# One constant in a delta-rule and MLP kernel: the input projection's eleven-product form in the last four blocks of tokens, in place of the last two

## The chip, the cores and the metric

The kernel runs on one core of a Trainium2 chip. The metric is the device time of one execution in microseconds (us), as the median of several runs. Engines are named TensorE (PE in the profile; PEld is its weight load), VectorE (DVE), ScalarE (ACT), GpSimd (POOL) and SyncE (SP, which here only issues DMAs).

## What is computed

A delta-rule recurrence over 4 batches, 8 heads, 768 tokens and 48 channels, and then an MLP with the hard-swish activation on the 3072 tokens, all in float32:

```python
k_n = k / (norm(k) + 1e-6)
for t in range(S):
    y[:, :, t] = q[:, :, t] @ state
    v_old = state^T k_n[t]
    state = state + beta[t] * outer(k_n[t], v[t] - v_old)
x = y.transpose(0, 2, 1, 3).reshape(3072, 384)
h = x @ w_in                                  # 384 -> 2048
g = h * clip(h + 3, 0, 6) / 6
out = g @ w_out                               # 2048 -> 384
```

## The kernel before

**Tokens and blocks.** The recurrence goes in 24 chunks t of 32 tokens, all batches at once on the 128 partitions. Each chunk needs the inverse of a triangular matrix; the chunks 1 to 4, 5 to 8, ... 17 to 20 and 21 to 23 form groups 1 to 6, and the inverse of a group is found by substitution on VectorE (`inverse(g)`): a transpose in (L456), 30 pairs of a product (L746) and a subtraction (L751) of growing and then shrinking size (128x30 up to 128x240 and back to 128x30), a memset (L755) and a transpose out (L460). Two chunks make a block of 256 tokens, `blk = t // 2`, and there are 12 blocks.

**The recurrence of one chunk** (`chain(t)`) has on TensorE: ks (L793, the state times keys and queries), pz (L814, the inverse X times the residual R), su (L912, the update of the state), py (L814, output), and yt (L859, the transposes of the output y into xT). Between them VectorE makes R (L806), y (L806, L849) and the new state (L928), and ScalarE copies.

**The MLP of one block** is "up" and "down". `up(blk)` multiplies 16 column tiles of `w_in`, three products of 128x256 each (L968); ScalarE (L976) and VectorE (L979) apply the activation and write g. `down_by_seven(blk)` multiplies g by `w_out` in Strassen's form with seven products (L1196); VectorE makes the sums of g (L1182, four groups named A22, A21, A11, A12), and combines the products (L1206); ScalarE copies them out of PSUM (L1203). The last instruction of down on VectorE is an L1206 that reads the last product.

**`up_by_eleven(blk)`**, used for blocks from `UF` on, does the 2x2 part of the projection (two column tiles of `w_in`, two halves of the tokens, the first two thirds of the 384 channels) in Strassen's form with seven products, and the last third plainly with four: eleven products of 128x128 (L1039) for each pair of column tiles, eight pairs to a block, where `up` has six of 128x256. It needs sums of `w_in` (`weight_sums`, 16 instructions on GpSimd, L1005, made during the down of block `UF - 1`; one of the sums overwrites tiles of `w_in`), and sums of x (`token_sums`, four instructions on VectorE, L1029, called T1x, T2x, T3x and T4x below; T1x is made first and used by the second product). For each pair of tiles, `begin` issues four products, a copy of them out of PSUM to g on ScalarE (L1053), and three additions on GpSimd (L1005); `end` issues the other seven products, two additions on VectorE (L1069, L1070), and then ScalarE's copy (L1076) and relu (L1080, into a buffer ro that shares its place with the output tile o) and VectorE's product (L1083), the last a pair behind.

**The order of the work** is written out by hand. From chunk 5 on each chunk has 15 units; in a unit u, `plan[u]` issues the next part of the recurrence, then one piece of the MLP (`units`: 14 for a down, 16 for an up), then evictions, then steps of the substitution (`fill`). So block 8's up runs beside chunk 18, its down beside chunk 19, block 9's up beside chunk 20, its down beside chunk 21, and inverse(6) is begun in chunk 18 and must be whole before pz of chunk 21. The lines that use the constant or follow from it:

```python
sums = weight_sums() if blk == UF - 1 else iter(())                     # L1284
(up_by_eleven if blk + 1 >= UF else up)(blk + 1)                        # in L1290
12: lambda: token_sums(t // CB) if t % CB and t // CB >= UF else None,  # L1435
take(fill, 1 if mode["slow"] else 2 + (u % 3 == 0))
```

`mode["slow"]` is set while an `up_by_eleven` runs, and what is left of a substitution when the next group of chunks begins is issued in one go (`drain(fill)`). Each engine works through its own instructions in that order.

Of the kernel before, what the change touches and what calls it, by code (L numbers as in the profile page):

```python
# [46 lines left out]
def kernel(  # L47
# [942 lines left out]
                past.add(("up", blk))  # L990
            yield

    UF = 10
    S1, S2, S4 = (sums_in[:, i] for i in range(3))

    def w_tiles(s, i):
# [10 lines left out]
    def weight_sums():  # L1007
        for j in range(0, NPR, 2):
            r = slice(j, j + 2)
            plus_minus(S1[:, r], W21[:, r], W22[:, r], ALU.add)  # L1010
            yield
            plus_minus(S2[:, r], S1[:, r], W11[:, r], ALU.subtract)
            yield
            plus_minus(S4[:, r], W12[:, r], S2[:, r], ALU.subtract)
            yield
            plus_minus(W21[:, r], W11[:, r], W21[:, r], ALU.subtract)
            yield
# [5 lines left out]
    def token_sums(blk):  # L1023
        needs(("seam", blk * CB), ("seam", blk * CB + 1), ("up", blk - 1))
        B11, B12, B21, B22, _, _ = (
            x.rearrange("p (a b) -> p a b", b=16) for x in x_tiles(blk)
        )
        for out, a, b in ((T1x, B12, B11), (T2x, B22, T1x), (B12, B22, B12), (T4x, B21, T2x)):
            nc.vector.tensor_tensor(out=out, in0=a, in1=b, op=ALU.subtract)  # L1029
        past.add(("sums", blk))  # L1030
# [230 lines left out]
    def mlp_units():  # L1261
# [10 lines left out]
        def downs(blk):  # L1272
            if blk >= FIRST:
                yield from down_by_seven(blk)
                return
            for c in range(CB):
                for f in range(0, NFC, WF):
                    if c == 0:
                        needs(*(("read", ("ph", blk, f + i, None)) for i in range(2)))
                    down(blk, c, f)  # L1280
                    yield

        for blk in range(1, N // CB):
            sums = weight_sums() if blk == UF - 1 else iter(())  # L1284
            for _ in downs(blk):
# [3 lines left out]
            if blk + 1 < N // CB:  # L1289
                for n, _ in enumerate((up_by_eleven if blk + 1 >= UF else up)(blk + 1)):  # L1290
                    if blk + 1 == FIRST and n >= HF:
# [10 lines left out]
    def take(gen, n=1):  # L1302
        for _ in range(n):
            while next(gen, None) == 1:
                pass
# [91 lines left out]
    with tc.manual_schedule():  # L1397
# [12 lines left out]
        for t in range(LS, N):  # L1410
# [11 lines left out]
            if i == 2:  # L1422
# [11 lines left out]
                11: lambda: take(ch),  # L1434
                12: lambda: token_sums(t // CB) if t % CB and t // CB >= UF else None,  # L1435
                13: lambda: take(later),
# [56 lines left out]
```

## Time and profile before

| what | value |
|---|---|
| time, median of 3 runs | 687.84 us (685.55 to 689.42) |
| time of the profiled execution | 685.55 us |
| its span, first to last instruction | 683.8 us |
| TensorE busy | 647.7 us (95%) |
| TensorE weight loads busy | 572.6 us (84%) |
| VectorE busy | 475.2 us (69%) |
| ScalarE busy | 253.3 us (37%) |
| GpSimd busy | 118.3 us (17%) |
| mean granted TensorE clock | 0.990 |

The span is the time from the first to the last instruction; 1.75 us lie around it. Shares of busy time are means over stages of different kinds, so the stages are read one by one. In the tables below a line such as "L1039 PE MATMUL ph<-xT,w_in" means that line 1039 issues a product on TensorE that writes the tile ph from xT and w_in; in a timeline the first number is the start in us from the start of the span, the second the duration, and a bracket at the end gives the idle time before the instruction and who ended it. A float32 product of TensorE counts as two records.

### The profile page before, as it was taken

To read this page: it belongs to the slowest core of one execution; us is meant where nothing else is said; L and a number is where in the kernel's file an instruction comes from. 1 tells how busy PE (TensorE), PEld (TensorE's weight loads), DVE (VectorE), ACT (ScalarE), POOL (GpSimd) and SP (SyncE) were. 2 spreads that over 40 slices of the span, in tenths; PEclk is the share of its full clock that TensorE was granted. 3 is DMA by queue.
4 is the path that set the end of the run, shared out by engine and by line. 5 is a ranking of instruction groups with operands and counts; after the bars stand their busy time and mean duration, and the time that the engine had idled before them with its cause. 6 is when DMAs were issued, how large, how long until landed. Compare 5 with 4: busy or idle time off the path is not lost.

```text
span 683.8 us, 25829 instructions
## 1 busy us (share of the span) xinstructions
PE 647.7 (95%) x11368; PEld 572.6 (84%) x11368; DVE 475.2 (69%) x1234; ACT 253.3 (37%) x503; POOL 118.3 (17%) x200
## 2 busy tenths in 40 slices
PE   2588989999999999999999999999999999999997
PEld 2468977776689989989988988978988989999997
DVE  5888867898556996746985746985546995457354
ACT  5986776423133133232133132132232132143250
POOL 6240232002311100100100101102000032040230
PEclk9997999999999999999999999999999999999999
DMA  7995435402040030041030030020020020100000
GB/s 182 246 215 132 99 88 130 80 4 45 23 86 14 3 72 2 3 89 19 2 71 2 3 71 2 2 61 2 3 47 2 3 48 2 28 11 2 25 1 23
DMA packets 88496, 33.23 MB, mean 49 GB/s; under 512 B 80160, under 2 KB 83232, under 8 KB 88384
## 3 DMA queue, kind: packets, MB, share of 16 engines
q1 hardware_dynamic: 88128, 31.29, 20.5%
q8 instruction: 89, 1.46, 0.9%
q10 hardware_dynamic: 256, 0.30, 0.2%
q14 instruction: 23, 0.19, 0.1%
HBM read 26.84 MB, written 4.72 MB: 46 GB/s over the span
## 4 chain that ended last, share of the span: by engine, by line
PE 78%; DVE 16%; issue 2%; ACT 2%; DMA 1%; SPq 0%; POOL 0%; DVEq 0%; ACTq 0%
PE ph L968 28%; PE po L1196 22%; PE ph L1039 6%; PE po L1131 4%; PE pt L513 3%; PE ks L793 3%; DVE g L1182 3%; PE py L814 3%; PE su L912 3%; PE pz L814 2%; DVE A L751 2%; DVE pr L746 2%; PE sc L534 2%; PE yt L859 1%; PE pi L671 1%
## 5 line engine op out<-in xcount | busy, mean ns | idle before, releaser
L968 PE MATMUL ph<-xT,w_in 128*128 128x256 f32 (+1 forms) x1056 | 227.4, 368 | 3.4 <-DVE g L979 2.8
L968 PEld LDWEIGHTS ph<-xT,w_in 128*128 128x128 f32 x1056 | 185.3, 194 | 27.7 <-DVE g L979 3.9
L976 ACT ACTIVATE g<-ph,halves 128x256 f32<-128x256 f32 (+1 forms) x176 | 79.1, 453 | 165.5 <-PE ph L968 163.4
L979 DVE SCALAR_TENSOR_TENSOR g<-g,ph 128x256 f32<-128x256 f32 (+1 forms) x176 | 68.1, 391 | 67.4 <-ACT g L976 67.2
L1196 PE MATMUL po<-w_out,g 128*128 128x192 f32 x640 | 112.1, 326 | 0.0
L1196 PEld LDWEIGHTS po<-w_out,g 128*128 128x128 f32 x640 | 104.7, 190 | 0.4
L1196 PE MATMUL po<-spare,g 128*128 128x192 f32 x480 | 86.7, 332 | 0.0
L1196 PEld LDWEIGHTS po<-spare,g 128*128 128x128 f32 x480 | 77.2, 190 | 1.8
L1182 DVE TENSOR_TENSOR g<-g 128x256 f32<-128x256 f32 x160 | 65.7, 459 | 3.3 <-PE po L1196 3.2
L473 POOL TENSOR_TENSOR mb<-beta_tok,mask 128x256 f32<-128x256 f32 x38 | 25.9, 702 | 236.8 <-DVE LB L545 236.8
L751 DVE TENSOR_TENSOR A<-A,pr 128x30 f32<-128x30 f32 (+9 forms) x150 | 53.7, 358 | 3.4
L746 DVE TENSOR_TENSOR pr<-A 128x30 f32<-128x30 f32 (+9 forms) x150 | 52.0, 347 | 3.1
L348 ACT ACTIVATE spare<-spare,places 128x768 uint16<-128x768 uint16 (+1 forms) x56 | 52.4, 940 | 2.9 <-DMA spare<-in_moe_w_in_dram 2.0
L1131 PE MATMUL po<-w_out,g 128*128 128x384 f32 x128 | 45.6, 493 | 0.0
L1203 ACT ACTIVATE o<-po 128x192 f32<-128x192 f32 x40 | 13.2, 330 | 82.4 <-PE po L1196 82.4
L521 ACT ACTIVATE KQ<-pt 128x512 f32<-128x512 f32 x48 | 28.1, 594 | 29.6 <-PE pt L513 29.2
L1039 PE MATMUL ph<-xT,w_in 128*128 128x128 f32 x224 | 34.2, 278 | 0.2
L497 POOL TENSOR_TENSOR kb<-kf,inv 128x384 f32<-128x384 f32 x24 | 22.3, 930 | 66.2 <-PE yt L859 35.6
L1131 PEld LDWEIGHTS po<-w_out,g 128*128 128x128 f32 x128 | 23.2, 190 | 12.4
L1005 POOL TENSOR_TENSOR g<-g 128x128 f32<-128x128 f32 x48 | 21.8, 455 | 67.8 <-ACT g L1053 65.3
L863 ACT ACTIVATE xT<-yt 128x384 f32<-128x384 f32 x24 | 11.7, 486 | 57.2 <-PE yt L859 57.2
L793 PEld LDWEIGHTS ks<-state,KQ 64*64 64x64 f32 x1472 | 24.8, 138 | 8.6 <-issue 7.7
(137 smaller groups left out, 779.7 us busy)
## 6 DMA issues: line engine op xcount, KB each, us to landing
kf<-in_k_dram SPq DMA_DIRECT2D x96, 48.0 KB, 2.7
qb<-in_q_dram SPq DMA_DIRECT2D x96, 48.0 KB, 2.9
vf<-in_v_dram SPq DMA_DIRECT2D x96, 48.0 KB, 2.1
out_dram<-o SPq DMA_DIRECT2D x92, 48.0 KB, 1.6
spare<-in_moe_w_in_dram SPq DMA_DIRECT2D x4, 768.0 KB, 7.6
w_out<-in_moe_w_in_dram SPq DMA_DIRECT2D x4, 768.0 KB, 7.1
w_out<-in_moe_w_out_dram SPq DMA_DIRECT2D x4, 768.0 KB, 6.6
spare<-in_moe_w_out_dram SPq DMA_DIRECT2D x4, 768.0 KB, 4.8
```

What stands on the lines that cost most here:

```text
L348: nc.scalar.activation(out=z, in_=z if n else d.bitcast(I16)[:, :, :, 3], func=func, bias=places[:, n : n + 1], scale=scale,)
L746: nc.vector.tensor_tensor(out=pv, in0=A[:, j + 1 :, j].unsqueeze(2).to_broadcast([n, w, j]), in1=A[:, j, 0:j].unsqueeze(1).to_broadcast([n ...
L751: nc.vector.tensor_tensor(out=A[:, j + 1 :, 0:j], in0=A[:, j + 1 :, 0:j], in1=pv, op=ALU.subtract)
L793: nc.tensor.matmul(ph[y][c, e, D * p : D * p + D], lhsT=KQ[r, p * B // 2 + b // 2, 2 * y : 2 * y + 2, :].rearrange("k y c -> k (y c)"), rh ...
L814: nc.tensor.matmul(ps[rows(place(b)), D * h : D * h + D], lhsT=m(h)[rows(b)], rhs=z[rows(b), D * h : D * h + D], start=True, stop=True, sk ...
L968: nc.tensor.matmul(ph[:, cols], lhsT=w_in[:, s, f * 128 : (f + 1) * 128], rhs=xT[:, s, cols], start=(s == 0), stop=(s == NKT - 1),)
L976: nc.scalar.activation(out=g, in_=ph, func=ACTF.Relu, bias=half, scale=1.0 / 6.0)
L979: nc.vector.scalar_tensor_tensor(out=g, in0=g, scalar=1.0, in1=ph, op0=ALU.min, op1=ALU.mult)
L1039: nc.tensor.matmul(ph[:, n], lhsT=w, rhs=x, start=start, stop=stop, skip_group_check=True)
L1131: nc.tensor.matmul(pos[c][:], lhsT=gs[blk, f // 2][:, f % 2, c * P : (c + 1) * P], rhs=w_out[:, f, :], start=(f == 0), stop=(f == NFC - 1),)
L1182: nc.vector.tensor_tensor(out=A(f, *out), in0=A(f, *a), in1=A(f, *b), op=op)
L1196: nc.tensor.matmul(ps[n][:], lhsT=A(f - f % 2, *a)[:, f % 2], rhs=b[:, f], start=(f == 0), stop=(f == HF - 1),)
```

## The change

The constant UF goes from 10 to 8:

```diff
@@ -990,7 +990,7 @@
                 past.add(("up", blk))
             yield
 
-    UF = 10
+    UF = 8
     S1, S2, S4 = (sums_in[:, i] for i in range(3))
```

With it, blocks 8 and 9 go through `up_by_eleven` in place of `up`; `weight_sums` is made during the down of block 7 in place of block 9; `token_sums` is made for blocks 8 and 9 too, in unit 12 of the chunks 17 and 19, one unit behind the last unit of a down; and the substitution of group 6 goes at one step a unit while block 8's and block 9's ups run. Nothing else is edited.

## The prediction

> **What bounds the kernel now.** TensorE is busy for 95% of the span. So I first read the table of stages, cut where TensorE goes from one block's first projection ("up", L968 or L1039) to its output projection ("down", L1196). Columns: length, then busy time and instruction count of TensorE, its weight loads, VectorE, ScalarE, GpSimd; granted clock; DMA.
>
> ```profile
> core 0: us, PE busy (x) PEld busy (x) DVE busy (x) ACT busy (x) POOL busy (x), PEclk, DMA share, GB/s
> ...
> 498.27:523.44 25.17, 25.17 (x358) 21.56 (x357) 11.90 (x28) 8.45 (x18) 0.00 (x0) 1.00 0.15 34
> 523.44:546.08 22.64, 22.64 (x373) 21.70 (x371) 20.82 (x64) 3.58 (x9) 0.00 (x0) 1.00 0.00 1
> 546.08:571.24 25.16, 25.16 (x356) 21.55 (x356) 21.45 (x55) 8.45 (x18) 9.38 (x13) 1.00 0.16 34
> ...
> 593.88:619.09 25.21, 24.62 (x438) 23.70 (x436) 13.23 (x34) 11.73 (x24) 10.86 (x24) 1.00 0.11 26
> ```
>
> These are up(8), down(8), up(9) and up(10). Three things are to be seen. TensorE fills every stage, so a stage lasts as long as its products. up(10), already in the form with eleven products, takes 25.21 us, no less than the plain up(8) with 25.17. And VectorE is nearly full in down(8), 20.82 of 22.64 us: that is inverse(6), the substitution of the last tokens.
>
> Why eleven products gain nothing, the timeline of TensorE at the start of up(10) tells (start, duration, what it waited for in brackets):
>
> ```profile
> 593.88 0.38 PE L1039 MATMUL ph<-xT,w_in 128*128 128x128 f32 x2
> 594.79 0.46 PE L1039 MATMUL ph<-beta_tok,sums_in 128*128 128x128 f32 x2 [0.52 <-DVE beta_tok L1029]
> 595.32 0.46 PE L1039 MATMUL ph<-xT,w_in 128*128 128x128 f32 x2
> ```
>
> A product of 128 columns then starts every 0.2233 us (11 in 2.456 us, 649.40 to 651.86), one of 256 columns every 0.433 us (six in 2.60 us, 520.84 to 523.44). 88 x 0.2233 = 19.65 against 48 x 0.433 = 20.78: 1.13 us less. But the second product waits for x's first sum (L1029), and VectorE makes that only after the last addition of the output (L1206): the first three products take 1.73 us (593.88 to 595.61) for 0.67, 1.06 lost. The rest goes in changes between instruction kinds.
>
> **Part by part.** In the two builds' orders, TensorE, ScalarE and GpSimd have up(8) and up(9) exactly in the shape of up(10), with the recurrence at the same places; SP's queue is the same.
>
> *Up(8), by the row of up(10): 25.21 - 25.17 = +0.04.* Its VectorE queue holds no substitution ahead of x's sums (down(7) has none). The transpose A<-L (1.97 us) falls into the idle 1.08 us ahead of a group's additions; the next group absorbs the rest. The 24 added additions on GpSimd (0.456 us each), the 24 copies and relus on ScalarE and the 8 x 3 VectorE instructions stand in up(10) beside TensorE, at no cost beyond the 25.21. ro and the output tile share one buffer, but the output's DMAs are issued as early as in up(10).
>
> *Down(8): VectorE starts late.* The plain up leaves VectorE free, so the first ten steps of the substitution ran at 523.19 to 526.53, ahead of the recurrence's R. With eleven products up's last VectorE instruction (L1083) starts 2.47 us after down's first product and lasts 0.60 (621.56 against 619.09, in up(10)). So the steps start at 523.48 + 3.07 = 526.55, and with 2.77 us (their pitches below) R is at 529.32, where it was at 527.23: 2.09 us late. Does that wash out?
>
> ```profile
> 523.19 0.20 DVE L746 TENSOR_TENSOR pr<-A 128x30 f32<-128x30 f32 x1
> ...
> 526.23 0.30 DVE L751 TENSOR_TENSOR A<-A,pr 128x130 f32<-128x130 f32 x1
> 527.23 0.74 DVE L806 SCALAR_TENSOR_TENSOR R<-ks,parity,vf 128x192 f32<-128x192 f32 x2 [0.70 <-PE ks L793]
> ...
> 542.05 0.55 DVE L849 TENSOR_TENSOR y<-y,py 128x384 f32<-128x384 f32 x1
> ...
> 546.45 0.35 DVE L1206 TENSOR_TENSOR o<-u,po 128x192 f32<-128x192 f32 x1
> 546.72 0.40 DVE L751 TENSOR_TENSOR A<-A,pr 128x238 f32<-128x238 f32 x1
> 547.16 0.40 DVE L746 TENSOR_TENSOR pr<-A 128x234 f32<-128x234 f32 x1
> 547.59 0.40 DVE L751 TENSOR_TENSOR A<-A,pr 128x234 f32<-128x234 f32 x1
> ```
>
> No: after 527.23 no wait is listed until 567.73. VectorE runs without a gap through down(8), so 2.09 us of lag reaches its end. In the new order, x's sums of block 9 stand where the instruction at 547.59 stands. Three effects:
>
> 1. y of token 19 ends at 542.60 + 2.09 = 544.69; its transposes (yt) are due at 544.45 + 0.04 and start 0.15 after y (443.34 + 0.55 to 444.04): 544.84, **+0.35**.
> 2. up(9)'s first product: 546.08 + 0.04 + 0.35 = 546.47. T1x starts at 547.59 + 2.09 = 549.68 and the second product 0.43 later (594.36 to 594.79), at 550.11: 3.64 us behind the first, where up(10) has 0.91. **+2.73**, and +0.05 for the stage (25.21 - 25.16).
> 3. The Strassen sums of down(8) (L1182) are late too, but have 3 to 4 us to spare (A12 ends at 540.37 + 2.09, read at 544.78): nothing.
>
> *Up(9) and down(9).* In up(9) substitution goes at one step a unit, 17 steps beside the additions; ten more, a memset and a transpose come at the end in one go. From the time of T1x on, by the rows of up(10): last L1083 ends at +27.8, the steps 2.77, memset and transpose 1.95, R 1.3: +33.8. TensorE, whose down(9) starts at +24.73, wants pz 9.17 later (580.41 - 571.24), at +33.9: **+0.1** for the latency. So the thinned substitution just fits.
>
> *GpSimd's weight sums* move from beside up(9) to beside up(7) and the start of down(7), 16 x 0.73 us; bkb of the last token, which nothing reads, is queued behind them. They stretch VectorE's two-input steps: one took 0.86 us at 551.98 beside them, its neighbours 0.33 to 0.37. In up(7) that makes VectorE some 2 us later around 467; y of token 16 (due by 471.04, made at 468.98) then ends near 470.9: 0 to +0.3, I take 0.
>
> [...]
>
> *The clock.* Effect 2 leaves TensorE idle from about 546.85 to 550.11, 3.26 us. What such a gap does, earlier windows of this trace show: 1.79 us idle (46.75 to 48.54, longest wait 1.79), and then
>
> ```profile
> 46.50:49.93 3.43, 1.64 (x101) 1.29 (x96) 3.29 (x6) 3.37 (x5) 2.12 (x5) 0.99 0.92 260
> 49.93:53.34 3.41, 2.79 (x67) 2.31 (x66) 3.34 (x6) 3.11 (x5) 0.00 (x0) 0.50 0.41 70
> 53.34:56.75 3.41, 3.41 (x17) 3.41 (x18) 3.03 (x13) 0.73 (x2) 0.00 (x0) 0.51 0.98 258
> ```
>
> the clock is halved for 6.8 us. After 1.66 us idle (91.34 to 93.00) it was halved from 94.2 to 97.7, while 1.18 us idle (454.5) did nothing. 3.26 us idle puts at least 1.63 into one stretch of 3.4 us. Ends: 0, and two stretches, 3.4 us; I take one stretch of 3.41 us at half clock, **+1.7**, nearest to the 1.66 us row.
>
> [...]
>
> **Sum.** 0.04 + 0.35 + 2.73 + 0.05 + 0.1 + 1.7 = +4.97 us. The profiled execution took 685.55 (span 683.8 and 1.75 around it), so 690.5 for it; it is the fastest of three, the median being 687.84. I set the sum on the middle of the two, 686.7: **691.7**.
>
> **Rivals.** (a) The clock stays up: +3.27, 690.0. For it: 1.18 us idle did nothing. Against: two gaps of 1.66 and 1.79 us both halved it. 0.23. (b) The lag is absorbed, because up(8)'s tail is shorter than up(10)'s or VectorE's waits give way: +0 to +1.5, some 687.5. Against it, VectorE's 40 us without a wait. 0.13. (c) GpSimd's additions hold up the 17 steps of up(9) by 0.51 us each (0.86 - 0.35), 8.7 us, where VectorE has 6.2 to spare (27.8 less 14.6 for x's sums, the additions and the recurrence, less 17 x 0.41): pz another 2.5 late, +7.5, 694.2. Against: GpSimd works only 60% of that time. 0.08. (d) The other side: x's sums of both blocks come early enough, so that each block keeps the 1.13 us: -2.3, 684.4. It decides if T1x is made before down's last product ends; the order of VectorE puts it behind, and up(10) and up(11) both waited. 0.04. My forecast: 0.52.
>
> **How the numbers follow.** Half a per cent (3.4 us, about what a measurement of this kernel can tell from no change) puts the bounds at 684.4 and 691.3. Slower: forecast, (c), a little of (a): 0.60. Faster: (d), 0.04. Same: 0.36. Range: from the middle of (b), 687.0, to past (c) and two slow stretches (695), 696.
>
> **What would show it.** Right: the second product of up(9) waits about 3 us for L1029 and the granted clock is 0.5 for some 3.4 us after it; up(8) takes about 25.2 us; R in down(8) comes 2 us later; pz of down(9) hardly waits. Wrong: a gap below 1.5 us at up(9), which would mean that VectorE had caught up; a full clock after the gap; or waits inside up(9), (c).

## The result, and the profile after

| | before | after |
|---|---|---|
| median, us | 688.4 (683.82 to 692.34, 20 runs) | 693.49 (688.65 to 697.9, 20 runs) |
| ratio after/before, 95% interval | | 1.0074 (1.0051 to 1.0098) |
| profiled execution, us | 685.55 | 689.89 |
| its span, us | 683.8 | 687.8 |
| mean granted TensorE clock | 0.990 | 0.985 |

The change makes the kernel slower by 0.74%, some 5 us. The forecast was slower, 691.7 us in a range of 687 to 696.

The table of stages of after, cut as that of before (length; busy time and count of TensorE, its weight loads, VectorE, ScalarE, GpSimd; clock; DMA). The lines are up(8), down(8), up(9), down(9) and up(10):

```profile
core 0: us, PE busy (x) PEld busy (x) DVE busy (x) ACT busy (x) POOL busy (x), PEclk, DMA share, GB/s
497.97:523.17 25.20, 24.61 (x437) 23.69 (x436) 15.02 (x35) 11.73 (x24) 10.97 (x24) 1.00 0.15 34
523.17:546.12 22.95, 22.84 (x373) 21.66 (x372) 21.03 (x64) 4.83 (x11) 0.00 (x0) 1.00 0.01 2
546.12:575.13 29.01, 25.98 (x437) 25.10 (x436) 20.82 (x57) 11.73 (x24) 11.03 (x24) 0.94 0.14 30
575.13:597.77 22.64, 22.64 (x373) 21.71 (x372) 17.30 (x49) 4.94 (x11) 0.00 (x0) 1.00 0.01 1
597.77:622.98 25.21, 24.65 (x437) 23.70 (x436) 12.88 (x34) 11.53 (x24) 10.90 (x24) 1.00 0.11 27
```

Against before, up(8) took 0.03 more, down(8) 0.31 more, up(9) 3.85 more, and down(9) and up(10) nothing. The tail after up(11) took 0.11 more (22.22 for 22.11). Together this is 4.3 us. Nine tenths of it stand in one stage, and the clock column shows the same stage: 0.94 in the mean.

TensorE at the start of up(9) in after (start, duration, bracket with idle time and releaser):

```profile
544.46 0.52 PE L859 MATMUL yt<-ident,y 128*128 128x128 f32 x3
...
546.12 0.38 PE L1039 MATMUL ph<-xT,w_in 128*128 128x128 f32 x2
549.53 0.79 PE L1039 MATMUL ph<-beta_tok,sums_in 128*128 128x128 f32 x2 [3.02 <-DVE beta_tok L1029]
550.15 0.77 PE L1039 MATMUL ph<-xT,w_in 128*128 128x128 f32 x2
```

The second product starts 3.41 us behind the first, after 3.02 us of idle time that ends with x's first sum. And the second and third product last 0.77 to 0.79 us, where before's up(10) had 0.46. That is the halved clock, which a cut of this stage into three parts shows:

```profile
546.12:549.40 3.28, 0.39 (x4) 0.19 (x2) 3.04 (x10) 0.00 (x0) 0.00 (x0) 1.00 0.06 16
549.40:552.82 3.42, 3.29 (x14) 3.20 (x15) 1.48 (x6) 0.60 (x1) 0.69 (x2) 0.50 0.37 100
552.82:575.13 22.31, 22.31 (x421) 21.71 (x420) 16.30 (x42) 11.14 (x23) 10.34 (x23) 1.00 0.11 21
```

One stretch of 3.4 us at half clock follows the idle stretch, then it is whole again.

Where x's sum was, VectorE's timeline in after tells, at the beginning and at the end of down(8):

```profile
525.64 0.69 DVE L1083 SCALAR_TENSOR_TENSOR g<-o,g 128x512 f32<-128x512 f32 x1 [0.85 <-ACT o L1080]
526.25 0.20 DVE L746 TENSOR_TENSOR pr<-A 128x30 f32<-128x30 f32 x1
...
528.96 0.74 DVE L806 SCALAR_TENSOR_TENSOR R<-ks,parity,vf 128x192 f32<-128x192 f32 x2
```

```profile
548.17 0.35 DVE L1206 TENSOR_TENSOR o<-u,po 128x192 f32<-128x192 f32 x1
548.44 0.40 DVE L751 TENSOR_TENSOR A<-A,pr 128x238 f32<-128x238 f32 x1
548.87 0.40 DVE L746 TENSOR_TENSOR pr<-A 128x234 f32<-128x234 f32 x1
549.19 0.28 DVE L1029 TENSOR_TENSOR beta_tok<-xT 128x128 f32<-128x128 f32 x1
```

The last L1083 of up(8) holds up the first ten steps of the substitution, and these hold up R, which starts 5.79 us into the stage (528.96 - 523.17) where before it was 3.79 (527.23 - 523.44): 2.00 us late. At the end of the stage x's first sum, T1x, stands behind the output's last addition and two more steps of the substitution, at 549.19.

**How executions are compared here.** The stages from about 370 us to the end of down(7) last the same in every profiled execution of this case, to 0.03 us. What lies before them does not: the first of these stages began between 369.59 and 375.02 us in the ten kernels, whose edits all act later. So single profiled spans differ by up to 5 us for no reason in the edit. Below, the stages from up(8) on are compared, and the whole time by the ratio from several runs.

### The profile page after: what moved, and what is told of

Its sections match the earlier page's. It is cut to its first block, busy times and chain, and to the rows that moved or that the text cites. A ratio compares the mean times of both kernels' runs of the same rounds, so it can differ in the third digit from the quotient of the medians.

```text
span 687.8 us, 26297 instructions
## 1 busy us (share of the span) xinstructions
PE 645.7 (94%) x11528; PEld 575.8 (84%) x11528; DVE 485.7 (71%) x1258; ACT 262.9 (38%) x519; POOL 140.3 (20%) x248
## 4 chain that ended last, share of the span: by engine, by line
PE 73%; DVE 19%; ACT 3%; issue 2%; DMA 1%; SPq 1%; DVEq 0%; ACTq 0%
PE ph L968 22%; PE po L1196 19%; PE ph L1039 12%; PE po L1131 4%; DVE g L1182 3%; DVE A L751 3%; DVE pr L746 3%; PE ks L793 3%; PE pz L814 2%; PE py L814 2%; PE su L912 2%; PE pt L513 2%; PE sc L534 2%; ACT spare L348 2%; DVE o L1206 1%
## 5 line engine op out<-in xcount | busy, mean ns | idle before, releaser
L968 PE MATMUL ph<-xT,w_in 128*128 128x256 f32 (+1 forms) x864 | 184.2, 366 | 5.3 <-DVE g L979 2.9
L968 PEld LDWEIGHTS ph<-xT,w_in 128*128 128x128 f32 x864 | 149.9, 195 | 24.9 <-DVE g L979 3.9
L976 ACT ACTIVATE g<-ph,halves 128x256 f32<-128x256 f32 (+1 forms) x144 | 64.2, 450 | 131.9 <-PE ph L968 131.8
L1196 PEld LDWEIGHTS po<-w_out,g 128*128 128x128 f32 x640 | 104.5, 190 | 0.3
L979 DVE SCALAR_TENSOR_TENSOR g<-g,ph 128x256 f32<-128x256 f32 (+1 forms) x144 | 55.0, 386 | 51.6 <-ACT g L976 51.3
L1005 POOL TENSOR_TENSOR g<-g 128x128 f32<-128x128 f32 x96 | 43.8, 458 | 145.7 <-ACT g L1053 140.6
L1039 PE MATMUL ph<-xT,w_in 128*128 128x128 f32 x448 | 70.0, 280 | 0.3
L1039 PEld LDWEIGHTS ph<-xT,w_in 128*128 128x128 f32 x448 | 59.7, 194 | 1.5 <-issue 0.8
L1053 ACT ACTIVATE g<-ph 128x512 f32<-128x512 f32 x32 | 19.1, 597 | 50.5 <-PE ph L1039 50.5
L1069 DVE TENSOR_TENSOR g<-ph,g 128x128 f32<-128x128 f32 x32 | 9.2, 289 | 36.1 <-POOL g L1005 22.4
```

What stands on the lines that cost most here:

```text
L968: nc.tensor.matmul(ph[:, cols], lhsT=w_in[:, s, f * 128 : (f + 1) * 128], rhs=xT[:, s, cols], start=(s == 0), stop=(s == NKT - 1),)
L976: nc.scalar.activation(out=g, in_=ph, func=ACTF.Relu, bias=half, scale=1.0 / 6.0)
L979: nc.vector.scalar_tensor_tensor(out=g, in0=g, scalar=1.0, in1=ph, op0=ALU.min, op1=ALU.mult)
L1005: nc.gpsimd.tensor_tensor(out=out, in0=a, in1=b, op=op)
L1039: nc.tensor.matmul(ph[:, n], lhsT=w, rhs=x, start=start, stop=stop, skip_group_check=True)
L1196: nc.tensor.matmul(ps[n][:], lhsT=A(f - f % 2, *a)[:, f % 2], rhs=b[:, f], start=(f == 0), stop=(f == HF - 1),)
```

## The experiments

The theory: the loss is one wait, at up(9)'s second product, and the halved clock that it brings. It has two causes: x's sums stand behind the addition that reads down's last product in VectorE's queue, and VectorE comes 2 us late to down(8). The rivals: GpSimd's 24 additions beside VectorE are what costs; or the clock has nothing to do with it and the wait alone does it; or the eleven products can't be had more cheaply than twelve. All times of stages are in us:

| kernel | up(8) | down(8) | up(9) | down(9) | up(10) | up(11) | ratio to before (95%) |
|---|---|---|---|---|---|---|---|
| before | 25.17 | 22.64 | 25.16 | 22.64 | 25.21 | 20.77 | 1 |
| after | 25.20 | 22.95 | 29.01 | 22.64 | 25.21 | 20.77 | 1.0074 (1.0051 to 1.0098) |
| e3_filler | 25.20 | 22.95 | 27.80 | 22.65 | 25.20 | 20.77 | 1.0025 (1.0005 to 1.0044) |
| e4_uf9 | 25.17 | 22.64 | 26.12 | 22.65 | 25.20 | 20.76 | 1.0009 (0.9991 to 1.0026) |
| e1_sums_ahead | 24.15 | 22.93 | 25.93 | 22.64 | 24.16 | 19.72 | 0.9971 (0.9950 to 0.9992) |
| e2_no_lag | 25.20 | 22.64 | 29.00 | 22.65 | 25.20 | 20.77 | 1.0044 (1.0024 to 1.0064) |
| e7_spread | 25.75 | 22.64 | 26.36 | 22.64 | 25.21 | 20.77 | 1.0029 (1.0010 to 1.0048) |
| e5_both | 24.70 | 22.65 | 26.71 | 22.64 | 24.16 | 19.72 | 0.9978 (0.9950 to 1.0006) |
| e6_sums_ahead_uf10 | 25.16 | 22.64 | 25.16 | 22.64 | 24.16 | 19.72 | 0.9964 (0.9940 to 0.9987) |
| e8_late | 24.15 | 22.65 | 25.00 | 22.65 | 24.15 | 19.72 | 0.9962 (0.9938 to 0.9987) |

Each was made from the changed kernel, but e6_sums_ahead_uf10 from the kernel before.

### e3_filler: the same wait with TensorE kept busy

```diff
-            mm(ph, 0, W11[:, j], B11, start=True)
+            for _ in range(14 if blk == 9 and j == 0 else 1):
+                mm(ph, 0, W11[:, j], B11, start=True)
```

The first product of up(9) is issued 14 times.

> The changed kernel, with the first product of up(9) issued 14 times instead of once (each run starts the sum anew, so that the value is the same). It fills the wait for T1x with 13 x 0.223 = 2.9 us of products that need nothing new. Theory (the wait lowers the clock): the second product starts at the same time as in the changed kernel, the granted clock stays at 1.00, up(9) takes 29.0 - 1.3 = 27.7 us, the time is the kernel before's +3.5 to +4 us. Rival (the products after the wait are slow for another reason, such as their reads): they are at 0.42 us again with work ahead of them, up(9) takes 29 us, +5 us.

TensorE's timeline in e3_filler, and the first 6.8 us of its up(9) in two halves:

```profile
548.21 3.29 PE L1039 MATMUL ph<-xT,w_in 128*128 128x128 f32 x28
551.62 0.49 PE L1039 MATMUL ph<-beta_tok,sums_in 128*128 128x128 f32 x2
552.24 0.46 PE L1039 MATMUL ph<-xT,w_in 128*128 128x128 f32 x2
```

```profile
548.21:551.62 3.41, 3.29 (x30) 3.10 (x29) 3.13 (x11) 0.00 (x0) 0.00 (x0) 1.00 0.08 22
551.62:555.03 3.41, 3.28 (x26) 3.12 (x27) 1.39 (x5) 1.19 (x2) 1.24 (x3) 1.00 0.38 100
```

The second product is 3.41 us behind the first, exactly as in after, but now the clock stays at 1.00: 26 records in the second half, where after had 14 at half clock. up(9) takes 27.80 for 29.01. So of the 3.85 us, 1.21 were the clock, and the rest, 2.64, is the wait with what else differs in the stage. It also shows that the idle time, and not the late sum as such, lowered the clock: the sum was as late here, and the clock 1.00 for after's 0.50. By the ratios e3_filler lies 0.49% below after, some 3.4 us where the stage gives 1.21. The two ratios are uncertain by about 0.2% each, so this is at the edge of what they allow; the sums by stage against before, 3.0 and 4.3 us, lie inside the two intervals.

### e4_uf9: block 9 alone

```diff
-    UF = 8
+    UF = 9
```

up(8) stays plain; up(9) has its eleven products.

> UF = 9: block 9 in the eleven-product form, block 8 plain as in the kernel before. Theory: without up(8)'s additions VectorE begins the substitution as early as in the kernel before, so down(8) has no lag, and T1x stands only behind the two steps queued between it and the last L1206: the second product of up(9) starts 1.9 us behind the first (wait 1.5 us), up(9) takes 26.2 us with a whole clock, 27.5 with a halved one, and down(8) 22.64. Time +1.1 us against the kernel before, or +2.4 where the clock falls (1.2 us idle did not lower it, 1.66 us did). Rival (each block in this form costs the same): half of the change's loss, +2.5 us, with a wait as in up(10), 0.5 us.

TensorE at the start of up(9) in e4_uf9, and the stage:

```profile
547.95 0.38 PE L1039 MATMUL ph<-xT,w_in 128*128 128x128 f32 x2
549.77 0.46 PE L1039 MATMUL ph<-beta_tok,sums_in 128*128 128x128 f32 x2 [1.44 <-DVE beta_tok L1029]
```

```profile
547.95:574.07 26.12, 24.61 (x436) 23.69 (x436) 19.46 (x52) 11.74 (x24) 10.99 (x24) 1.00 0.15 33
```

With up(8) plain VectorE is on time: R starts 3.79 us into down(8), as before (529.10 - 525.31), and down(8) takes its 22.64. The second product still comes 1.82 us behind the first, 0.91 more than in up(10): 0.74 of these are the two steps of the substitution that stand between the last L1206 and T1x in chunk 19, and not in chunk 21 (1.02 us from the one to the other for 0.28), and 0.17 come from the last L1206, which starts that much later behind the first product. The other 1.59 of after's 3.41 come from the lag: T1x starts 26.02 us into down(8) in after (549.19 - 523.17) and 24.03 in e4_uf9 (549.34 - 525.31), 1.99 late. The later first product of up(9) has taken 0.31 of it, and the second product followed T1x by 0.34 us here and by 0.43 there. And 1.44 us of idle time left the clock whole (1.00) in this execution. The time is the same as before, within what is measured.

### e1_sums_ahead: x's sums one unit earlier

```diff
-                11: lambda: take(ch),
-                12: lambda: token_sums(t // CB) if t % CB and t // CB >= UF else None,
+                11: lambda: (take(ch), token_sums(t // CB) if t % CB and t // CB >= UF else None),
```

> The changed kernel, with x's sums (L1029) put one unit earlier, ahead of the last unit of the down instead of behind it, in all four blocks with eleven products. Theory (the loss is the wait for the first sum T1x, and the half clock that follows the long wait in block 9): the waits of 0.5 us in up(8), up(10) and up(11) go, about 0.9 us each with the slow restart, 2.7 us in all; in up(9) T1x is made some 1.9 us earlier, so that the wait falls from 3.0 to about 1.2 us and the clock stays whole, 1.9 + 1.3 us. Against the kernel before: +5 - 2.7 - 3.2 = about -1 us, each up near 24.3 us and up(9) near 25.8. Rival (the form with eleven products is itself slower, by its small products and more work on the other engines): the ups stay at 25.2 and 29 and the time at +4 to +5 us.

TensorE at the start of up(8), and the second product of up(9), in e1_sums_ahead:

```profile
502.06 0.38 PE L1039 MATMUL ph<-xT,w_in 128*128 128x128 f32 x2
502.28 0.39 PE L1039 MATMUL ph<-beta_tok,sums_in 128*128 128x128 f32 x2
...
550.68 0.49 PE L1039 MATMUL ph<-beta_tok,sums_in 128*128 128x128 f32 x2 [1.15 <-DVE beta_tok L1029]
```

In up(8), up(10) and up(11) the wait is gone, and each gains 1.05 us: the second product follows 0.22 us behind the first. So that wait was what ate the gain of eleven products. In up(9), where VectorE comes late, 3.02 us of waiting became 1.15, and the clock stayed whole (1.00 in the stage): 25.93. down(8) keeps its extra 0.3. One line moved turns a loss of 5 us into a gain of 2. The 24 additions on GpSimd are all still there in up(8), beside 24.15 us: they are not what costs there, and that rival falls. (In up(9), where the substitution runs beside them, they stretch its steps, as the next run shows.)

### e2_no_lag: no substitution right ahead of x's sums, two steps a unit later

```diff
-                if i == 1 == ready[0] and 5 < u < 12:
+                if i == 1 == ready[0] and 5 < u < 12 or t == 19 and 7 < u < 13:
                     continue
-                take(fill, 1 if mode["slow"] else 2 + (u % 3 == 0))
+                take(fill, 1 if mode["slow"] and t < 19 else 2 + (u % 3 == 0 and not mode["slow"]))
```

In chunk 19 no steps go in the units 8 to 12, and from there on two go in each unit of block 9's up. The ten steps ahead of R stay where they are.

> The changed kernel, in which the substitution of group 6 makes no step in units 8 to 12 of chunk 19, ahead of x's sums of block 9, and two steps a unit in chunk 20 in place of one. Theory (VectorE's lag through down(8) makes T1x late): VectorE has caught up when down(8) ends, T1x comes as early as in up(10), the wait at the start of up(9) is 0.5 us, the clock stays at 1.00, up(9) takes 25.2 to 25.6 us, and the time is the kernel before's +0 to +1 us. Rival (GpSimd's additions hold up VectorE's steps in up(9)): with twice the steps there, up(9) has waits inside or pz of down(9) comes 2 us or more late, and the time stays at +3 us or more.

The start went as this theory had it: down(8) took 22.64, and the wait at up(9)'s second product was 0.43. But up(9) still took 29.00. VectorE's and TensorE's timelines in the middle of up(9), and the clock after it, in e2_no_lag:

```profile
567.65 0.60 DVE L746 TENSOR_TENSOR pr<-A 128x184 f32<-128x184 f32 x1
568.28 0.50 DVE L751 TENSOR_TENSOR A<-A,pr 128x184 f32<-128x184 f32 x1
...
570.52 0.55 DVE L849 TENSOR_TENSOR y<-y,py 128x384 f32<-128x384 f32 x1
```

```profile
571.12 0.83 PE L859 MATMUL yt<-ident,y 128*128 128x128 f32 x3 [1.95 <-DVE y L849]
571.75 0.64 PE L1039 MATMUL ph<-xT,w_in 128*128 128x128 f32 x2
```

```profile
547.26:576.26 29.00, 26.49 (x437) 25.35 (x436) 23.90 (x61) 12.06 (x24) 12.12 (x24) 0.94 0.14 30
...
572.00:573.00 1.00, 1.00 (x6) 1.00 (x6) 0.93 (x4) 0.68 (x2) 0.00 (x0) 0.50 0.00 0
```

The steps that were moved met GpSimd's additions: a step of 128x184 took 0.50 to 0.60 us, where the second one took 0.34 in e8_late (566.09), with GpSimd idle. VectorE was busy 23.90 us with the stage, y of chunk 20 came late, its transposes waited 1.95 us, and the clock was halved from 571.2 to 574.7. Ahead of that y stand 22 steps in up(9), where after has 12, and eleven of them are stretched, by an estimate 2.0 us together (against steps of the same size that met no addition). So my expectation for the time failed, and the rival's mechanism was seen, together with the ten more steps: VectorE has not the time for both in up(9), and work that is moved there comes back as a wait for something else, with the same halved clock.

### e7_spread and e5_both: the steps spread out evenly

```diff
-                if i == 1 == ready[0] and 5 < u < 12:
+                if i == 1 == ready[0] and 5 < u < 12 and t != 18 or (t, u) == (19, 0):
                     continue
-                take(fill, 1 if mode["slow"] else 2 + (u % 3 == 0))
+                take(fill, 4 if t == 19 and u > 11 else 1 if mode["slow"] or t == 18 else 2 + (u % 3 == 0 and t != 19))
```

e7_spread starts the substitution earlier, beside up(8), and takes fewer steps in down(8). e5_both has this and e1_sums_ahead's move.

> The changed kernel with the steps of the substitution of group 6 spread otherwise, x's sums where the change has them: one step a unit from unit 6 of chunk 18 on (beside up(8)), none in unit 0 of chunk 19 and two a unit to unit 11, four a unit in units 12 to 14 (beside the start of up(9), where VectorE idles 3.7 us in the changed kernel), one a unit in chunk 20. Theory (VectorE's lag from the end of up(8) through down(8) is the cause): R of chunk 19 is on time, yt does not wait, T1x stands only behind the two steps queued ahead of it, so that the second product of up(9) waits 1.4 us as with UF = 9, the clock stays whole, and down(8) takes 22.64 and up(9) 26.1 us; against the changed kernel 0.3 + 2.9 = 3.2 us less, +1 us against the kernel before. Rival (the steps in up(8) and up(9) collide with GpSimd's additions wherever they are): yt or pz wait by 1 us or more, and the gain is given back.

> Both cures together: the steps spread as in the run with spread steps, and x's sums one unit earlier in all four blocks. Theory: no wait for x's sums is left, the four ups take 24.15, 24.2, 24.15 and 19.72 us, down(8) 22.64; against the kernel before 1.0 us less in each of the four, -4.1 us (0.994), since 88 products of 0.2233 us take 1.1 us less than 48 of 0.433. Rival (two of these savings come out of one wait): up(9) stays near 25.9, -2 us.

In e7_spread the wait of up(9) shrank to 1.19 us and the clock stayed whole (1.00 in its 26.36 us), but up(8) lost 0.55: there too y of the recurrence now comes late (25.75, with 0.28 of idle time that y ended). e5_both shows where the rest went. Two of TensorE's waits in its up(9), and the stage:

```profile
561.60 1.03 PE L814 MATMUL pz<-R,X 32*32 32x48 f32 x64 [1.09 <-DVE R L806]
...
573.00 0.49 PE L1039 MATMUL ph<-xT,w_in 128*128 128x128 f32 x2 [0.68 <-DVE y L849]
```

```profile
550.74:577.45 26.71, 24.71 (x437) 23.73 (x437) 23.58 (x61) 11.73 (x24) 12.07 (x24) 1.00 0.16 32
```

No wait for x's sums is left in up(9), yet it takes 26.71, more than e1_sums_ahead's 25.93: R and y come late in its place, as VectorE is busy 23.58 of 26.71 us. I had expected 4.1 us less than before; that failed (0.9978, with 1 inside the interval).

### e6_sums_ahead_uf10: the earlier sums in the kernel before

UF is 10 again, with e1_sums_ahead's move.

> The kernel before (UF = 10) with x's sums one unit earlier in its two blocks with eleven products: what the earlier sums alone are worth. Theory: up(10) 24.15 and up(11) 19.72 us in place of 25.21 and 20.77, nothing else changes, -2.1 us (0.997). Rival (the gain of the earlier sums with UF = 8 came from blocks 8 and 9): no change.

up(10) and up(11) in e6_sums_ahead_uf10:

```profile
595.45:619.61 24.16, 24.16 (x438) 23.56 (x436) 13.41 (x35) 11.74 (x24) 10.90 (x24) 1.00 0.12 27
...
641.44:661.16 19.72, 19.72 (x177) 19.72 (x177) 10.06 (x26) 10.41 (x21) 10.90 (x24) 1.00 0.08 21
```

Both are shorter by 1.05 us and without idle time, as expected. The move alone makes the kernel before faster by 0.36%.

### e8_late: the earlier sums, and the steps where VectorE has room

```diff
-                take(fill, 1 if mode["slow"] else 2 + (u % 3 == 0))
+                late = {6: 2, 9: 1, 10: 1, 11: 1, 12: 3, 13: 3, 14: 2} if t == 19 else {}
+                take(fill, late.get(u, 1 if mode["slow"] else 2 + (u % 3 == 0)))
```

This has e1_sums_ahead's move too. In chunk 19 fewer steps stand ahead of T1x and more behind it.

> UF = 8 with x's sums one unit earlier, and with five steps of the substitution moved from chunk 19's units 6 and 9 to 11 (ahead of x's sums of block 9) to its units 12 to 14 (behind them, where VectorE waits 3.7 us for the first additions in the changed kernel); all other steps as in the change. Theory (what is left of the loss in that form is VectorE's lag of about 2 us): T1x of block 9 comes before it is wanted, up(9) takes 24.2 us in place of 25.93 and down(8) 22.7, R and y of chunk 20 have room for the later steps; -4 us against the kernel before (0.994). Rival (VectorE has no room left in up(9), as the runs with more steps there suggest): R, y or pz wait by as much as T1x gains, up(9) stays above 25.5, -2 us.

TensorE at the start of up(9), and its only listed wait in that stage, in e8_late:

```profile
547.70 0.39 PE L1039 MATMUL ph<-xT,w_in 128*128 128x128 f32 x2
547.92 0.39 PE L1039 MATMUL ph<-beta_tok,sums_in 128*128 128x128 f32 x2
...
568.25 0.49 PE L1039 MATMUL ph<-xT,w_in 128*128 128x128 f32 x2 [0.27 <-DVE y L849]
```

No wait for x's sums is listed in any of the four blocks. From up(8) to the end it takes 3.2 us less than before (up(8) 1.02, up(9) 0.16, up(10) 1.06, up(11) 1.05, less 0.05 in down and tail), by the ratio 0.38% or 2.6 us. It beats both kernels, the kernel before by less than the 4 us that I had expected. Its up(9) still takes 25.00, not 24.15, and the 0.85 us are lost at two places. The third product starts 0.48 us behind the second (547.92 to 548.40), where e1_sums_ahead's up(8) has 0.22 (502.28 to 502.50): in the kernel it reads T3x, the third of x's sums, and VectorE made that at 547.97 to 548.25. From there on the stage runs 0.32 us behind e1_sums_ahead's up(8). The wait for y, 0.27 us as listed, brings 0.54 more, read at the transposes (569.25, 21.55 us into the stage, where e1_sums_ahead's up(8) has 522.75, 20.69). That it is better than e6_sums_ahead_uf10 (0.9964), the intervals do not show.

## Why the prediction was right, step by step

- **Up(8), +0.04:** 0.03. Right, by the row of up(10); the gain of eleven products is eaten by the wait for T1x, which e1_sums_ahead shows by taking it away.
- **VectorE 2.09 us late at R, and no recovery in down(8):** 2.00 us, and it reached the end of the stage. Right. e4_uf9, where up(8) is plain, has no lag. (The last L1083 lasts 0.69 us in the trace, not 0.60. What counts is when the next instruction starts, 0.61 later in after, 525.64 to 526.25.)
- **yt of chunk 19 (the prediction's "token 19"), +0.35:** down(8) took 0.31 more. The transposes start 0.14 us after y ends (543.77 + 0.55 to 544.46), 21.29 us into the stage for 21.01 before. Right, though the wait is too short to be listed.
- **The Strassen sums of down(8), 0:** right, no wait for them is listed. The spare time was smaller than said: by the prediction's own figures A12 would end at 542.46 and be read at 544.78, 2.3 us and not 3 to 4.
- **Start of up(9), +2.73:** the second product was 3.41 us behind the first, not 3.64, so +2.50. The mechanism is right, the size 0.23 too large: T1x came 26.02 us into down(8), not 26.20 (549.68 - 523.48), 0.09 of it because the lag was 2.00 and not 2.09, and the product followed T1x by 0.34 us, not by 0.43. VectorE made up nothing of its lag: against e4_uf9 T1x is 1.99 us late.
- **One stretch of 3.41 us at half clock, +1.7:** one stretch, from 549.40 to 552.82, and +1.21 by e3_filler, or 1.30 as what the stage holds beyond 25.21 + 2.50. This is the most mis-sized term. I had taken half of the stretch as lost. But its first 0.13 us were still the wait (549.40 to 549.53), and at this place TensorE did not reach its full rate even with a whole clock: the 26 records that e3_filler fits into 3.41 us are 2.90 us of products at 0.2233 us a pair. After did 14 of them, 12 less, 1.34 us of products, and without the 0.13 some 1.21. That the clock fell at all was less sure than the rows chosen made it look. The same trace of before has a wait of 1.05 us (65.39 to 66.44) with a halved stretch behind it (66.93 to 70.35), which the prediction did not consider, and in e3_filler a wait of 2.23 us left the clock whole (last section). The length of the wait did not settle it, so that it came as forecast is in part luck. The prediction's 1.63 us supposes that idle time counts by stretches of 3.41 us. That was an estimate from the length of the halved stretches in before (49.93 to 53.34, 66.93 to 70.35), and no run tested it.
- **The 17 steps just fit in up(9); down(9) +0.1:** down(9) took 22.64, nothing more. Only four steps met the additions, and took 0.50 to 0.52 us for 0.31 to 0.37, a stretch of at most 0.2 us and not the 0.51 of rival (c), so VectorE had room enough. The 0.51 was read beside the weight sums (0.73 us each), not beside the shorter additions (0.46, 24 in 11.03 us). e2_no_lag shows the other side: with two steps a unit there it has not.
- **GpSimd's weight sums beside up(7), 0:** y of chunk 16 came 1.5 us later in its stage (expected: some 2), no wait for it is listed, and up(7) and down(7) last as in all the kernels.
- **The sum, +4.97:** by stages 4.3, by the medians 5.1. The difference of these two lies within what the early part of the kernel varies by from one execution to the next, so it is chance that 4.97 lies nearer to 5.1 than to 4.3: by the stages the sum was 0.7 too large, nearly all of it in the clock and the start of up(9). That the forecast of 691.7 lies 1.8 below the median of 693.49 comes from the base: I set the sum on 686.7, and the median of before over 20 runs is 688.4.
- **Rivals:** (a), the clock stays up, is what e3_filler had to make artificially. (b), the lag is absorbed, did not happen. (d), the gain of 1.13 us a block, needed x's sums before down's last product ends, and with e1_sums_ahead's move it came nearly whole, 1.05 us; the change as it stands does not make that.

## What to carry to other kernels

A form with fewer products pays only if what its first products need is ready when they are due: here a sum of 0.28 us, one unit too late in VectorE's queue, cost all of the 1.05 us that a block saves. Work that is added ahead of a nearly full engine's queue shows up where that engine's last result of the stage is waited for (in down(8) VectorE was busy 21.03 of 22.95 us, and its lag of 2.00 us reached the end), and moving other work out of the way only pays where the engine has room: e2_no_lag and e5_both each took one wait away and got others. A wait on TensorE such as those here, of 1.05 to 3.02 us, is to be priced with and without a halved clock behind it, in up(9) 1.21 us more (after against e3_filler) or nothing.

## What the runs showed of the hardware that I had not expected

- **The length of a wait alone did not tell whether the clock was halved.** In the stages compared above 1.15 us (e1_sums_ahead), 1.19 (e7_spread) and 1.44 us (e4_uf9) left it whole, and 1.95 us (e2_no_lag) and 3.02 us (after) halved it for about 3.4 us. But the early part of the same traces has cases against any bound between. One wait before L793, the prediction's 1.66 us, is there in other runs too. Here it is in before, e3_filler and e6_sums_ahead_uf10, each with a stretch that follows it; and last, from before, a wait of 1.05 us and its stretch:

```profile
93.00 0.37 PE L793 MATMUL ks<-state,KQ 64*64 64x48 f32 x10 [1.66 <-issue]
94.24:97.65 3.41, 3.41 (x76) 3.04 (x76) 1.29 (x5) 2.77 (x6) 0.00 (x0) 0.50 0.00 0
...
94.74 0.37 PE L793 MATMUL ks<-state,KQ 64*64 64x48 f32 x10 [2.23 <-issue]
94.74:101.60 6.86, 6.50 (x169) 5.24 (x168) 4.89 (x10) 4.95 (x10) 2.77 (x3) 1.00 0.02 5
...
94.30 0.37 PE L793 MATMUL ks<-state,KQ 64*64 64x48 f32 x10 [2.22 <-issue]
95.26:98.67 3.41, 3.41 (x77) 3.04 (x76) 1.05 (x5) 2.54 (x6) 0.00 (x0) 0.50 0.02 5
...
66.44 0.78 PE L671 MATMUL pi<-X,sums_in 32*32 32x16 f32 x64 [1.05 <-DVE sums_in L689]
66.93:70.35 3.42, 3.42 (x97) 3.04 (x86) 3.42 (x11) 1.78 (x5) 0.92 (x3) 0.50 0.36 68
```

  2.22 us halved it and 2.23 us did not, and 1.05 us did, with another 0.48 us of waiting shortly ahead of it (64.18 to 64.66). What else decides, such as where the wait falls or the shorter waits around it, was not tried, and stays open.
- **Products that only filled the gap kept the clock at 1.00.** 13 repeated products, in time that was lost anyway, gained 1.21 us in up(9) (e3_filler against after).
- **GpSimd's additions stretched the substitution's steps on VectorE less than its weight sums did:** 0.50 to 0.60 us for about 0.34 at 128x184 beside additions of some 0.5 us (24 in 12.12 us, e2_no_lag), where the row of before beside weight sums of 0.73 us showed 0.86 for 0.35. Other rows of before show the same (0.85 at 554.40, 0.87 for 0.30 at 558.11).
